# Converting float64 weights beside attention: sign of the weights, centring and the second weight matrix moved to other engines and another time

## The chip, the cores and the metric

The kernel runs on one core of one Trainium2 chip. Its time is the device time of one execution in microseconds (us), taken as the median of several runs. PE is the matrix engine, DVE is VectorE, ACT is ScalarE, POOL is GpSimd, SP is the engine that issues most DMAs.

## The reference

Threshold attention is followed by a Fourier mixing layer and a channel MLP. Everything is float32 but the two weight matrices, which arrive as float64.

```python
# q, k, v: (8 batches, 8 heads, 576 rows, 64);  tau: one number
scores = (q @ k.T) / sqrt(64)
scores = where(scores >= max(scores) - tau, scores, -1e9)
attn = softmax(scores) @ v                       # per head
x = attn, heads side by side                     # (8, 576, 512)
u = x + real(fft(fft(x, axis=1), axis=2))
un = (u - mean(u)) / sqrt(var(u) + 1e-6)         # over the 512 channels
out = u + relu(un @ w_ch1) @ w_ch2               # w_ch1 (512, 2048), w_ch2 (2048, 512), float64
```

## The kernel before, in words

**Attention** is a loop over 160 row steps `i`: 8 batches of 20 steps, a batch being 4 pairs of heads (`n`) with 5 row tiles (`t`) each, four of 128 rows and one of 64. A step has these parts. `scores(i)`: PE computes the scores of both heads into PSUM (`sc`, L319), VectorE takes the negated row maximum (`neg`, L332) and the threshold (`thr`, L336), ScalarE takes the exponential (`e`, L342), VectorE masks it and sums the row (L345), adds 1e-9 and inverts the sum (`den`, L349 and L352), and GpSimd repeats the inverse along a tile (`rec`, L354). `transposed_weights(i - 1)`: PE transposes the previous step's `e` and `rec` (L387, L392, L393), and ScalarE copies them out of PSUM. At the end of a pair `weighted_values` multiplies with the values (L409, L416) and GpSimd folds the rows for the Fourier transform (`fold`, L433 to L435). `e` and `rec` have two buffers.

**Mixing and channels.** After each batch, `mixing(b)` does the Fourier transforms as matmuls with tables of cosines and sines (`dim_c`, `dim_s`, `seq_c`, `seq_s`), and GpSimd adds the result to `x` into a ring `u_t` of two slots of 576 columns (L509 to L513). `channels(g)` then handles groups of 384 rows: 64 matmuls with `w1` (`ph`, L561), ReLU into `h0` to `h3`, a transpose of the rows for the mean and variance (`pn`), and 48 matmuls with `w2` (`po`, L582). This work is cut into units and handed out by `fill()`, three times a step during the next batch, by a budget of matmul columns; what is left runs at the end.

**Weights.** `weights()` is a generator over 32 chunks of 128 x 512: 16 of `w1` (four column groups `g` of four row blocks `c`), then 16 of `w2`. Each step takes two chunks (L640), so the program has them all handed out in the first 16 or 17 steps. `load_weights` reads a chunk as pairs of 32-bit words and builds the float32 value: VectorE masks the mantissa bits (L225), ScalarE makes 1 + mantissa of them (L228), VectorE adds the low word (L229), VectorE cuts out the exponent (L234), ScalarE shifts its bias and place (L238), VectorE puts the sign bit on (L241), and GpSimd multiplies the mantissa by this signed power of two (L245). The staging tiles, 128 x 1536, lie in the four `h` buffers, which `channels` uses later.

**Centring.** After each column group of `w1`, `center(g)` lets PE compute the column mean (`pm`, L253), ScalarE copies it (`mean`, L257), and VectorE subtracts it from each of the four blocks (L264). Blocks with odd `c` are mirrored first by a matmul (`pr`, L262), so VectorE reads those from PSUM.

**Start.** SP issues the loads of the first pair (`load_pair(0)`, 13 DMAs) and of `tau`; VectorE derives four scalars from `tau` (L142 to L154). `load_dim` loads the table `dim_raw`, in one of the two `e` buffers, by two DMAs on GpSimd's queue (L175, L177), and VectorE copies it in 25 pieces into `dim_c` and `dim_s` (L179 to L189).

The order within each engine's queue is chosen by a scheduler over the whole program, by its own model of times; it isn't the order of the source.

Of the kernel before, what the change touches and what calls it, by code (L numbers as in the profile page):

```python
# [9 lines left out]
FP32 = mybir.dt.float32  # L10
INT32 = mybir.dt.int32
UINT32 = mybir.dt.uint32
# [35 lines left out]
def kernel(  # L48
# [44 lines left out]
    def load_pair(n):  # L93
        b, p = n // NPAIR, PAIRS[n % NPAIR]
        hs = [2 * p + (j + p) % 2 for j in range(2)]
        qt = sb.tile([128, NT, 2, D], FP32, tag="q", bufs=1, name="q_in")
        kt = sb.tile([128, NT, 2, D], FP32, tag="k", bufs=1, name="k_in")
        vt = sb.tile([128, 9, D], FP32, tag="v", name="v_in")
        for j, h in enumerate(hs):
            nc.sync.dma_start(  # L100
                out=qt[:, 0:4, j, :], in_=q[b, h, 0:512, :].rearrange("(t p) d -> p t d", p=128)
            )
            nc.sync.dma_start(out=qt[0:64, 4, j, :], in_=q[b, h, 512:576, :])


        h = hs[0]
        nc.sync.dma_start(
            out=kt[:, 0:4, 0, :], in_=k[b, h, 0:512, :].rearrange("(t p) d -> p t d", p=128)
        )
        nc.sync.dma_start(out=kt[0:64, 4, 0, :], in_=k[b, h, 512:576, :])  # L110
        h = hs[1]
        nc.sync.dma_start(out=kt[0:64, 0, 1, :], in_=k[b, h, 512:576, :])
        rows = k[b, h, 0:512, :].rearrange("(t r p) d -> p r t d", r=2, p=64)
        nc.sync.dma_start(out=kt[64:128, 0:4, 1, :], in_=rows[:, 0])
        nc.sync.dma_start(out=kt[0:64, 1:5, 1, :], in_=rows[:, 1])

        for j, h in enumerate(hs):
            nc.sync.dma_start(
                out=vt[:, j:8:2, :], in_=v[b, h, 0:512, :].rearrange("(t p) d -> p t d", p=128)
            )  # L120
            nc.sync.dma_start(out=vt[64 * j : 64 * j + 64, 8, :], in_=v[b, h, 512:576, :])
        loaded[n] = (qt, kt, vt)

    load_pair(0)

# [12 lines left out]

    tau_t = const.tile([128, 1], FP32, name="tau_t")
    nc.sync.dma_start(out=tau_t[:, :], in_=tau.partition_broadcast(128))  # L140
    q_scale = const.tile([128, 1], FP32, name="q_scale")
# [48 lines left out]

    load_dim()

    w1 = [const.tile([128, HID], FP32, name=f"w1_{c}") for c in range(ND)]
# [17 lines left out]

    def load_weights(n, src, dst):

        if src.dtype == FP32:
            nc.sync.dma_start(out=dst, in_=src)
            return
        stage = sb.tile([128, 3 * WC], INT32, tag=f"h{n % 4}", bufs=1, name="stage")
        raw = stage[:, 0 : 2 * WC]
        power = stage[:, 2 * WC : 3 * WC]
        nc.sync.dma_start(out=raw, in_=src.bitcast(INT32))  # L220
        pairs = raw.rearrange("p (n two) -> p n two", two=2)
        low, high = pairs[:, :, 0].bitcast(UINT32), pairs[:, :, 1]
        bits = dst.bitcast(INT32)
# [5 lines left out]
        nc.vector.scalar_tensor_tensor(  # L229
            out=dst, in0=low, scalar=2.0**-52, in1=dst, op0=ALU.mult, op1=ALU.add  # L230
        )


        nc.vector.tensor_scalar(  # L234
            out=power, in0=high, scalar1=20, scalar2=0x7FF,
            op0=ALU.logical_shift_right, op1=ALU.bitwise_and,
        )
        nc.scalar.activation(  # L238
            out=power, in_=power, func=ACT.Relu, bias=shift[:, :], scale=float(1 << 23)
        )  # L240
        nc.vector.scalar_tensor_tensor(  # L241
            out=power, in0=high, scalar=-(1 << 31), in1=power,
            op0=ALU.bitwise_and, op1=ALU.bitwise_or,
        )
        nc.gpsimd.tensor_tensor(out=dst, in0=dst, in1=power.bitcast(FP32), op=ALU.mult)  # L245

    def center(g):
# [8 lines left out]
        mean = sb.tile([128, WC], FP32, tag="u", bufs=3, name="mean")  # L256
        nc.scalar.copy(mean[:, :], pm[:, :])  # L257
        for c in range(ND):
            rows = w1[c][:, cols]
            if c % 2:  # L260
                pr = ps.tile([128, 512], FP32, tag="mm", name="pr")
                nc.tensor.matmul(pr[:, :], mirror[:, :], rows, start=True, stop=True)  # L262
                rows = pr[:, :]
            nc.vector.tensor_tensor(  # L264
                out=w1[c][:, cols], in0=rows, in1=mean[:, :], op=ALU.subtract
            )

    def weights():
        n = 0
        for g in range(HID // WC):  # L270
            cols = slice(WC * g, WC * (g + 1))
            for c in range(ND):
                load_weights(n, w_ch1[128 * c : 128 * (c + 1), cols], w1[c][:, cols])
                n += 1
                yield
            center(g)
        for j in range(NJ):
            load_weights(n, w_ch2[128 * j : 128 * (j + 1), :], w2[j][:, :])
            n += 1
            yield  # L280
# [253 lines left out]
    def channels(g):  # L534
# [23 lines left out]
        for j in range(NJ):  # L558
# [15 lines left out]
            if j == 11:  # L574
                nc.scalar.activation(
                    out=rstd[:, :], in_=mv[:, :, 1], func=ACT.Sqrt, bias=eps[:, :], scale=1.0
                )
                nc.vector.reciprocal(rstd[:, :], rstd[:, :])
        for t in range(nt):
            po = ps.tile([128, DM], FP32, tag="mm", name="po")  # L580
# [47 lines left out]
    for i in range(total + 1):  # L628
# [9 lines left out]
        if i > 0 and t == 0:  # L638
            weighted_values(n - 1)
        for _ in itertools.islice(chunks, 2):  # L640
            pass
# [61 lines left out]
```

## Time and profile before

| | |
|---|---|
| median of 7 runs | 1923.44 us (1921.28 to 1925.78) |
| profiled execution | 1922.82 us, span 1921.0 us |
| mean granted TensorE clock | 0.975 |
| busy: PE, DVE, ACT, POOL | 1844.2, 869.4, 612.3, 237.1 us |

The span runs from the first to the last instruction that the profiler recorded. A group of instructions is shown as line, engine, operation, output and input tiles with partitions x elements and type, count, then busy us and the mean ns of one, then the idle time just before them on that engine and which instruction ended it. In a view of the timeline the first number is the start in us from the span's start and the second the length in us. Busy times of different engines overlap.

### The profile page before, as it was taken

How to read it: one execution, taken by the hardware profiler on the slowest of the kernel's cores; microseconds unless marked ns; L12 is line 12 of the kernel's file. 1: busy time of each engine (PE TensorE's matmuls, PEld its weight loads, DVE VectorE, ACT ScalarE, POOL GpSimd, SP SyncE). 2: the span in 40 equal slices, each digit the busy share in tenths (PEclk: the TensorE clock that was granted, in tenths of full speed). 3: DMA queues.
4: the chain of work that ended last, by engine and by line, in shares of the span. 5: the costliest groups of instructions: out<-in, count | busy, mean ns of one | idle time of the engine just before them, and what ended most of it. 6: DMA issues, size and time to landing. Idle time of an engine off the chain costs nothing.

```text
span 1921.0 us, 20963 instructions
## 1 busy us (share of the span) xinstructions
PE 1844.2 (96%) x7840; PEld 992.6 (52%) x7840; DVE 869.4 (45%) x2015; ACT 612.3 (32%) x1110; POOL 237.1 (12%) x438
## 2 busy tenths in 40 slices
PE   5877899999999999999999999999999999999999
PEld 3444555455455555545455455545555455545454
DVE  6998554533334545443333445544434355431010
ACT  3554443333223334323223234322323233421010
POOL 3433201010000210011000020002000020001000
PEclk9877899999999999999999999999999999999999
DMA  5432100100010010110001010101000001000000
GB/s 154 136 111 75 25 19 19 37 18 19 11 27 23 25 25 14 31 30 7 19 24 23 14 31 13 32 23 25 13 26 17 24 19 25 1 11 6 11 6 16
DMA packets 129701, 56.97 MB, mean 30 GB/s; under 512 B 120677, under 2 KB 120678, under 8 KB 129600
## 3 DMA queue, kind: packets, MB, share of 16 engines
q1 hardware_dynamic: 129232, 54.71, 10.7%
q8 instruction: 62, 1.02, 0.2%
q0 software_dynamic: 368, 0.93, 0.2%
q14 instruction: 39, 0.32, 0.1%
HBM read 46.02 MB, written 9.44 MB: 29 GB/s over the span
## 4 chain that ended last, share of the span: by engine, by line
PE 85%; DVE 10%; ACT 1%; POOL 1%; issue 1%; SPq 0%; DMA 0%; DVEq 0%; ACTq 0%
PE po L582 26%; PE ph L561 25%; PE sc L319 10%; PE pv L409 7%; PE pw L387 6%; PE pa L491 3%; PE pt L296 2%; DVE neg L332 2%; PE pv L416 2%; PE py L474 2%; DVE e L345 2%; DVE stage L241 1%; DVE w L229 1%; PE pe L392 1%; DVE w L225 1%
## 5 line engine op out<-in xcount | busy, mean ns | idle before, releaser
L582 PE MATMUL po<-w,h 128*128 128x512 f32 x1152 | 539.5, 606 | 0.0
L561 PE MATMUL ph<-u_t,w 128*128 128x384 f32 x1536 | 528.7, 493 | 5.4 <-DVE h L569 3.3
L342 ACT ACTIVATE e<-sc,neg 128x576 f32<-128x576 f32 (+1 forms) x320 | 229.2, 740 | 582.9 <-DVE neg L332 579.3
L561 PEld LDWEIGHTS ph<-u_t,w 128*128 128x128 f32 x1536 | 280.7, 190 | 207.3 <-issue 22.5
L332 DVE TENSOR_REDUCE neg<-sc 128x1 f32<-128x576 f32 (+1 forms) x320 | 229.6, 750 | 331.3 <-PE sc L319 330.9
L582 PEld LDWEIGHTS po<-w,h 128*128 128x128 f32 x1152 | 204.9, 190 | 229.8 <-issue 224.4
L319 PE MATMUL sc<-kT,qT 64*128 64x288 f32 (+1 forms) x1280 | 260.0, 450 | 35.9 <-ACT e_t L390 19.3
L345 DVE SCALAR_TENSOR_TENSOR e<-sc,thr,e 128x576 f32<-128x576 f32 (+1 forms) x320 | 250.7, 813 | 30.2 <-ACT e L342 12.7
L319 PEld LDWEIGHTS sc<-kT,qT 64*128 64x128 f32 (+1 forms) x1280 | 128.6, 183 | 167.3 <-issue 95.9
L390 ACT COPY e_t<-pw 128x1024 f32<-128x1024 f32 (+1 forms) x160 | 148.3, 927 | 160.1 <-PE pw L387 154.9
L354 POOL COPY rec<-den 128x128 f32<-128x128 f32 (+1 forms) x160 | 49.9, 312 | 1101.3 <-DVE den L352 932.5
L387 PEld LDWEIGHTS pw<-ident,e 128*128 128x128 f32 (+1 forms) x1280 | 141.6, 146 | 72.3 <-issue 55.1
L387 PE MATMUL pw<-ident,e 128*128 128x128 f32 (+1 forms) x1280 | 168.3, 275 | 0.1
L567 ACT ACTIVATE h<-ph 128x384 f32<-128x384 f32 x96 | 47.2, 492 | 314.7 <-PE ph L561 314.7
L569 DVE TENSOR_SCALAR h<-ph 128x384 f32<-128x384 f32 x96 | 53.3, 555 | 185.2 <-PE ph L561 184.9
L420 DVE TENSOR_TENSOR x<-pv,ends 128x288 f32<-128x288 f32 x64 | 29.2, 457 | 191.1 <-PE pv L416 174.4
L589 DVE SCALAR_TENSOR_TENSOR u<-po,rstd,u 128x512 f32<-128x512 f32 x36 | 27.0, 750 | 157.2 <-PE po L582 157.2
L409 PE MATMUL pv<-e_t,v_in 128*64 128x288 f32 x512 | 72.1, 419 | 0.0
L409 PE MATMUL pv<-e_t,v_rev 128*64 128x288 f32 x512 | 71.3, 418 | 0.1
L394 ACT COPY ends<-pe 128x256 f32<-128x256 f32 (+1 forms) x160 | 57.1, 357 | 3.0 <-PE pe L393 3.0
L409 PEld LDWEIGHTS pv<-e_t,v_in 128*64 128x64 f32 x512 | 34.8, 138 | 37.7 <-issue 10.3
L409 PEld LDWEIGHTS pv<-e_t,v_rev 128*64 128x64 f32 x512 | 34.5, 138 | 37.1 <-issue 11.1
(98 smaller groups left out, 1262.7 us busy)
## 6 DMA issues: line engine op xcount, KB each, us to landing
stage<-in_moe_w_ch_dram SPq DMA_DIRECT2D x32, 512.0 KB, 4.1
out_dram<-u SPq DMA_DIRECT2D x36, 256.0 KB, 2.0
q_in<-in_q_dram SPq DMA_DIRECT2D x64, 128.0 KB, 2.4
v_in<-in_v_dram SPq DMA_DIRECT2D x64, 128.0 KB, 2.4
k_in<-in_k_dram SPq DMA_DIRECT2D x32, 128.0 KB, 2.4
k_in<-in_k_dram SPq DMA_DIRECT2D x64, 64.0 KB, 2.4
q_in<-in_q_dram SPq DMA_DIRECT2D x64, 16.0 KB, 2.4
k_in<-in_k_dram SPq DMA_DIRECT2D x64, 16.0 KB, 2.1
```

What stands on the lines that cost most here:

```text
L319: nc.tensor.matmul(sc[j][0:m, c, 0:HALF], qT[hp, 128 * t : 128 * t + m], kT[hp, HALF * c : HALF * (c + 1)], start=True, stop=True,)
L332: nc.vector.tensor_reduce(out=neg[0:m, j : j + 1], in_=sc[j][0:m, :, 0:HALF], axis=AXIS_XY, op=ALU.max, negate=True,)
L342: nc.scalar.activation(out=ej, in_=sc[j][0:m, :, 0:HALF], func=ACT.Exp, bias=neg[0:m, j : j + 1], scale=1.0)
L345: nc.vector.scalar_tensor_tensor(out=ej, in0=sc[j][0:m, :, 0:HALF], scalar=thr[0:m, j : j + 1], in1=ej, op0=ALU.is_ge, op1=ALU.mult, accum ...
L387: nc.tensor.transpose(pw[:, 4 * j + c, 0:m], e[0:m, c0 : c0 + 128], ident[0:m, 0:m])
L390: nc.scalar.copy(e_t[:, :, qs], pw[:, :, 0:m])
L394: nc.scalar.copy(ends[:, :, qs], pe[:, 0:2, 0:m])
L409: nc.tensor.matmul(pv[64 * j : 64 * j + 64, 0:HALF], vt[:, 2 * c + j, :], e_t[:, 4 * j + c, cols], start=(c == 0), stop=False, skip_group_ ...
L491: nc.tensor.matmul(pa[0:m, 0:KH], y[0:n, u, cols], table[0:n, u, :], start=(u == 0), stop=(u == 2),)
L561: nc.tensor.matmul(ph[:, 0:GT], w1[c][:, 128 * j : 128 * (j + 1)], u_t[:, c, c0 : c0 + GT], start=(c == 0), stop=(c == ND - 1),)
L569: nc.vector.tensor_relu(ht, ph[:, 0:GT])
L582: nc.tensor.matmul(po[:, :], hT[j // 4][:, j % 4, 128 * t : 128 * (t + 1)], w2[j][:, :], start=(j == 0), stop=(j == NJ - 1),)
```

## The change

1. **Sign.** VectorE no longer puts the sign bit on. GpSimd multiplies the mantissa by the unsigned power of two, ScalarE computes Sign of the high word (`high`, in place, as float32), and GpSimd multiplies by that in a second operation. The power now lies in the words of `low`, so a staging tile is 128 x 1024.
2. **Centring.** ScalarE stores the negated mean. For odd blocks PE adds it to the mirrored block by a second matmul into `pr`, and ScalarE copies the sum to `w1`. For even blocks GpSimd adds it.
3. **When.** A step takes one chunk in the first 20 steps and two after that. A `w2` chunk is staged in the second slot of the ring `u_t` (two buffers), no longer in the `h` buffers. Before its `w2` matmuls, `channels` takes what chunks are left.
4. **Queues and tables.** `tau` and the five loads of the first pair's `k` are issued by ScalarE. `load_dim` is called in step 7, no longer ahead of the loop.

```diff
@@ -96,6 +96,8 @@
         qt = sb.tile([128, NT, 2, D], FP32, tag="q", bufs=1, name="q_in")
         kt = sb.tile([128, NT, 2, D], FP32, tag="k", bufs=1, name="k_in")
         vt = sb.tile([128, 9, D], FP32, tag="v", name="v_in")
+
+        k_queue = nc.sync if n else nc.scalar
         for j, h in enumerate(hs):
             nc.sync.dma_start(
                 out=qt[:, 0:4, j, :], in_=q[b, h, 0:512, :].rearrange("(t p) d -> p t d", p=128)
@@ -104,15 +106,15 @@
 
 
         h = hs[0]
-        nc.sync.dma_start(
+        k_queue.dma_start(
             out=kt[:, 0:4, 0, :], in_=k[b, h, 0:512, :].rearrange("(t p) d -> p t d", p=128)
         )
-        nc.sync.dma_start(out=kt[0:64, 4, 0, :], in_=k[b, h, 512:576, :])
+        k_queue.dma_start(out=kt[0:64, 4, 0, :], in_=k[b, h, 512:576, :])
         h = hs[1]
-        nc.sync.dma_start(out=kt[0:64, 0, 1, :], in_=k[b, h, 512:576, :])
+        k_queue.dma_start(out=kt[0:64, 0, 1, :], in_=k[b, h, 512:576, :])
         rows = k[b, h, 0:512, :].rearrange("(t r p) d -> p r t d", r=2, p=64)
-        nc.sync.dma_start(out=kt[64:128, 0:4, 1, :], in_=rows[:, 0])
-        nc.sync.dma_start(out=kt[0:64, 1:5, 1, :], in_=rows[:, 1])
+        k_queue.dma_start(out=kt[64:128, 0:4, 1, :], in_=rows[:, 0])
+        k_queue.dma_start(out=kt[0:64, 1:5, 1, :], in_=rows[:, 1])
 
         for j, h in enumerate(hs):
             nc.sync.dma_start(
@@ -121,6 +123,8 @@
             nc.sync.dma_start(out=vt[64 * j : 64 * j + 64, 8, :], in_=v[b, h, 512:576, :])
         loaded[n] = (qt, kt, vt)
 
+    tau_t = const.tile([128, 1], FP32, name="tau_t")
+    nc.scalar.dma_start(out=tau_t[:, :], in_=tau.partition_broadcast(128))
     load_pair(0)
 
 
@@ -136,8 +140,6 @@
 
 
 
-    tau_t = const.tile([128, 1], FP32, name="tau_t")
-    nc.sync.dma_start(out=tau_t[:, :], in_=tau.partition_broadcast(128))
     q_scale = const.tile([128, 1], FP32, name="q_scale")
     nc.vector.tensor_scalar(
         out=q_scale[:], in0=tau_t[:], scalar1=0.0, scalar2=SCALE, op0=ALU.is_ge, op1=ALU.mult
@@ -188,8 +190,6 @@
                     c, f, n = c + 1, f + step, n - 1
                 nc.vector.tensor_copy(dim_s[:, c : c + n], _stepped(raw, 256 + f, step, n))
 
-    load_dim()
-
     w1 = [const.tile([128, HID], FP32, name=f"w1_{c}") for c in range(ND)]
     w2 = [const.tile([128, DM], FP32, name=f"w2_{j}") for j in range(NJ)]
 
@@ -209,17 +209,18 @@
     shift = const.tile([128, 1], FP32, name="shift")
     nc.vector.memset(shift[:], -float((1023 - 127) << 23))
 
-    def load_weights(n, src, dst):
+    def load_weights(src, dst, raw):
+
 
         if src.dtype == FP32:
             nc.sync.dma_start(out=dst, in_=src)
             return
-        stage = sb.tile([128, 3 * WC], INT32, tag=f"h{n % 4}", bufs=1, name="stage")
-        raw = stage[:, 0 : 2 * WC]
-        power = stage[:, 2 * WC : 3 * WC]
-        nc.sync.dma_start(out=raw, in_=src.bitcast(INT32))
-        pairs = raw.rearrange("p (n two) -> p n two", two=2)
-        low, high = pairs[:, :, 0].bitcast(UINT32), pairs[:, :, 1]
+        nc.sync.dma_start(
+            out=raw, in_=src.bitcast(INT32).rearrange("p (c n) -> p c n", c=2)
+        )
+        pairs = raw.rearrange("p c (n two) -> p c n two", two=2)
+        low, high = pairs[:, :, :, 0], pairs[:, :, :, 1]
+        dst = dst.rearrange("p (c n) -> p c n", c=2)
         bits = dst.bitcast(INT32)
 
         nc.vector.tensor_scalar(
@@ -227,22 +228,21 @@
         )
         nc.scalar.activation(out=dst, in_=bits, func=ACT.Copy, bias=1.0, scale=2.0**-20)
         nc.vector.scalar_tensor_tensor(
-            out=dst, in0=low, scalar=2.0**-52, in1=dst, op0=ALU.mult, op1=ALU.add
+            out=dst, in0=low.bitcast(UINT32), scalar=2.0**-52, in1=dst, op0=ALU.mult, op1=ALU.add
         )
 
 
         nc.vector.tensor_scalar(
-            out=power, in0=high, scalar1=20, scalar2=0x7FF,
+            out=low, in0=high, scalar1=20, scalar2=0x7FF,
             op0=ALU.logical_shift_right, op1=ALU.bitwise_and,
         )
         nc.scalar.activation(
-            out=power, in_=power, func=ACT.Relu, bias=shift[:, :], scale=float(1 << 23)
-        )
-        nc.vector.scalar_tensor_tensor(
-            out=power, in0=high, scalar=-(1 << 31), in1=power,
-            op0=ALU.bitwise_and, op1=ALU.bitwise_or,
-        )
-        nc.gpsimd.tensor_tensor(out=dst, in0=dst, in1=power.bitcast(FP32), op=ALU.mult)
+            out=low, in_=low, func=ACT.Relu, bias=shift[:, :], scale=float(1 << 23)
+        )
+        nc.gpsimd.tensor_tensor(out=dst, in0=dst, in1=low.bitcast(FP32), op=ALU.mult)
+        sign = high.bitcast(FP32)
+        nc.scalar.activation(out=sign, in_=high, func=ACT.Sign)
+        nc.gpsimd.tensor_tensor(out=dst, in0=dst, in1=sign, op=ALU.mult)
 
     def center(g):
 
@@ -254,29 +254,32 @@
                 pm[:, :], ones[:, :], w1[c][:, cols], start=(c == 0), stop=(c == ND - 1)
             )
         mean = sb.tile([128, WC], FP32, tag="u", bufs=3, name="mean")
-        nc.scalar.copy(mean[:, :], pm[:, :])
+        nc.scalar.mul(mean[:, :], pm[:, :], -1.0)
         for c in range(ND):
             rows = w1[c][:, cols]
             if c % 2:
                 pr = ps.tile([128, 512], FP32, tag="mm", name="pr")
-                nc.tensor.matmul(pr[:, :], mirror[:, :], rows, start=True, stop=True)
-                rows = pr[:, :]
-            nc.vector.tensor_tensor(
-                out=w1[c][:, cols], in0=rows, in1=mean[:, :], op=ALU.subtract
-            )
+                nc.tensor.matmul(pr[:, :], mirror[:, :], rows, start=True, stop=False)
+                nc.tensor.matmul(pr[:, :], ident[:, :], mean[:, :], start=False, stop=True)
+                nc.scalar.copy(rows, pr[:, :])
+            else:
+                nc.gpsimd.tensor_tensor(out=rows, in0=rows, in1=mean[:, :], op=ALU.add)
 
     def weights():
         n = 0
         for g in range(HID // WC):
             cols = slice(WC * g, WC * (g + 1))
             for c in range(ND):
-                load_weights(n, w_ch1[128 * c : 128 * (c + 1), cols], w1[c][:, cols])
+                stage = sb.tile([128, 2, WC], INT32, tag=f"h{n % 4}", bufs=1, name="stage")
+                load_weights(w_ch1[128 * c : 128 * (c + 1), cols], w1[c][:, cols], stage[:, :, :])
                 n += 1
                 yield
             center(g)
+
         for j in range(NJ):
-            load_weights(n, w_ch2[128 * j : 128 * (j + 1), :], w2[j][:, :])
-            n += 1
+            c = 2 * (j % 2)
+            raw = u_t[:, c : c + 2, S : S + WC].bitcast(INT32)
+            load_weights(w_ch2[128 * j : 128 * (j + 1), :], w2[j][:, :], raw)
             yield
 
 
@@ -576,6 +579,8 @@
                     out=rstd[:, :], in_=mv[:, :, 1], func=ACT.Sqrt, bias=eps[:, :], scale=1.0
                 )
                 nc.vector.reciprocal(rstd[:, :], rstd[:, :])
+        for _ in chunks:
+            pass
         for t in range(nt):
             po = ps.tile([128, DM], FP32, tag="mm", name="po")
             for j in range(NJ):
@@ -637,7 +642,9 @@
         fill()
         if i > 0 and t == 0:
             weighted_values(n - 1)
-        for _ in itertools.islice(chunks, 2):
+        if i == 7:
+            load_dim()
+        for _ in itertools.islice(chunks, 1 if i < per_batch else 2):
             pass
         if i > 0 and i % per_batch == 0:
             b = i // per_batch - 1
```

## The prediction

> **What bounds the kernel now.** I read the page's shares and its 40 slices first, to see whether one engine bounds the whole span.
>
> ```profile
> PE 1844.2 (96%) x7840; PEld 992.6 (52%) x7840; DVE 869.4 (45%) x2015; ACT 612.3 (32%) x1110; POOL 237.1 (12%) x438
> ...
> PE   5877899999999999999999999999999999999999
> ...
> DVE  6998554533334545443333445544434355431010
> ```
>
> A slice is 48 us. PE is full from the sixth slice on; only in the first four (195 us) is it not, and there VectorE shows 6, 9, 9, 8. All that the change touches lies in these slices and the one or two behind them, so the second view is the windows over that stretch.
>
> ```profile
> core 0: us, PE busy (x) PEld busy (x) DVE busy (x) ACT busy (x) POOL busy (x), PEclk, DMA share, GB/s
> 0.00:50.00 50.00, 29.68 (x95) 16.81 (x96) 35.18 (x95) 20.07 (x31) 17.11 (x33) 0.93 0.56 154
> 50.00:100.00 50.00, 42.77 (x175) 22.45 (x173) 49.23 (x103) 28.39 (x46) 20.09 (x21) 0.87 0.48 141
> 100.00:150.00 50.00, 36.86 (x150) 21.02 (x150) 47.00 (x94) 26.02 (x42) 18.53 (x18) 0.68 0.36 109
> 150.00:195.00 45.00, 34.77 (x162) 20.66 (x161) 36.91 (x76) 22.17 (x35) 14.53 (x16) 0.75 0.24 65
> 195.00:250.00 55.00, 50.48 (x252) 30.51 (x254) 28.75 (x68) 20.86 (x39) 11.70 (x21) 0.88 0.08 17
> 250.00:300.00 50.00, 49.80 (x263) 28.53 (x262) 28.34 (x69) 21.59 (x43) 4.24 (x11) 1.00 0.09 19
> ```
>
> VectorE is busy 49.2 of 50 us, then 47.0 of 50: the first batch (20 row steps) is VectorE's. Up to 195 us it works 168.3 us, ScalarE 96.7, GpSimd 70.3, and PE idles 50.9. From 250 us on PE has no room. A microsecond saved on VectorE before 195 us is a microsecond off the span as long as nothing else is late; one saved after 250 us is nothing. The timeline puts the first `neg` (L332) of step 1 at 16.9, of step 16 at 170.8 and of step 20 at 194.9 us: with conversions a step takes 10.3 us, without them (steps 16 to 19) 6.0.
>
> The third view is the groups of lines up to 195 us.
>
> ```profile
> L241 DVE SCALAR_TENSOR_TENSOR stage<-stage 128x512 int32<-128x512 int32 x32 | 29.3, 916 | 0.0
> L229 DVE SCALAR_TENSOR_TENSOR w<-stage,w 128x512 f32<-128x512 uint32 x32 | 23.3, 728 | 0.8 <-ACT w L228 0.7
> L234 DVE TENSOR_SCALAR stage<-stage 128x512 int32<-128x512 int32 x32 | 22.8, 714 | 0.0
> L225 DVE TENSOR_SCALAR w<-stage 128x512 int32<-128x512 int32 x32 | 19.0, 593 | 0.4 <-DMA stage<-in_moe_w_ch_dram 0.4
> L264 DVE TENSOR_TENSOR w<-w,mean 128x512 f32<-128x512 f32 x8 | 5.4, 679 | 0.4 <-ACT mean L257 0.4
> L264 DVE TENSOR_TENSOR w<-pr,mean 128x512 f32<-128x512 f32 x8 | 5.4, 678 | 0.0
> ...
> L245 POOL TENSOR_TENSOR w<-w,stage 128x512 f32<-128x512 f32 x32 | 46.6, 1456 | 57.6 <-DVE stage L241 44.7 <-DVE den L352 12.9
> ...
> L238 ACT ACTIVATE stage<-stage,shift 128x512 int32<-128x512 int32 x32 | 22.9, 716 | 18.3 <-DVE stage L234 14.4 <-DMA stage<-in_moe_w_ch_dram 2.3 <-DVE den L352 0.9
> ```
>
> These means hide a second length. In the timeline of VectorE and GpSimd around 30 us:
>
> ```profile
> 30.46 1.64 POOL L245 TENSOR_TENSOR w<-w,stage 128x512 f32<-128x512 f32 x1 [0.62 <-DVE stage L241]
> ...
> 30.90 1.48 DVE L234 TENSOR_SCALAR stage<-stage 128x512 int32<-128x512 int32 x1
> ...
> 32.64 0.41 DVE L234 TENSOR_SCALAR stage<-stage 128x512 int32<-128x512 int32 x1
> ```
>
> The same L234 takes 0.41 us when GpSimd is free and 1.48 us beside its multiplication: VectorE is held until GpSimd ends. So GpSimd's work has a price on VectorE, and the change gives GpSimd twice as much of it.
>
> **The sum, part by part.** Times go against the profiled execution (1922.8 us, span 1921.0; the median of the runs, 1923.4, is 0.6 above). In the instruction order of the changed kernel as built, PE, VectorE, ScalarE and GpSimd run as before from about step 25 on, so only the first 250 us can differ.
>
> *Off VectorE.* Sign insertion L241, 29.3 us; centring L264, 10.8; and the w2 chunks that leave the first batch. That order moves only five of the 16 past step 20 (w2_11 to w2_15); eleven are still converted in the first batch. Five times 593 + 714 + 728 ns is 10.2. Together −50.3.
>
> *More holding by GpSimd.* Each chunk now has two multiplications, and centring adds 8 additions: in the first batch 27 × 2 + 8 = 62 operations for 32. At 1456 ns that is 90 us for 46.6; of a first batch of 154 us before and some 135 after, the share goes from 0.30 to 0.67, 2.2 times. The holds that remain exposed are those on L234, 32 × (714 − 410) = 9.7, L225, 32 × (593 − 410) = 5.9, and L229, 32 × (728 − 680) = 1.5 (medians 418, 422 and 680 ns): 17.1, for 27 chunks 14.4. Times 2.2 is 31.7: +17, and +2 for `thr` (211 ns free, mean 279): +19. No hold growing gives 0; each operation holding as now, 0.83 us, gives +35 (rival B).
>
> *GpSimd's own queue.* `rec` (L354), for which PE's transpose of it (L393) waits each step, now queues behind two multiplications: up to 1.5 us more a step, 29 us in all. Its cover is PE's 50.9 us of idle time: 0, and if it is gone, those 29.
>
> *PE, ScalarE.* Eight matmuls more, by L262's eight (16 records, 9.1 us busy), in the same idle time: 0. ScalarE gets 32 Signs, of which no row shows one; bounds from L228 (627) and L238 (716 ns) are 20 to 23 us, and 8 PSUM copies at L257's 581 ns, 4.6: 97 becomes 125 of some 180 us. It is not the bound: 0. If Sign needed another table than Exp, each pair of switches would be 2 × 1.28 us (ACT_TABLE_LOAD L305); the built order has no second load before the first batch ends: 0.
>
> *Start.* The `tau` wait on VectorE (10.5 us) goes, but the first L225, L229 and L234 now stand ahead of step 0's `neg` and wait for the first weight load, which SP still issues: 0, ±2.
>
> *dim table at step 7.* The 24 copies are moved, same cost. `dim_raw` takes one of the two `e` buffers and has two DMAs on GpSimd's queue with 4.0 us to landing; VectorE's copies wait behind them, then the next steps' `e`: up to 8 us, the DMA alone 4: +4.
>
> *Loads.* L225 of chunk n needs the load into the buffer that GpSimd's last multiplication of chunk n−4 frees; that is later now, and a load takes 4.1 us. 0 to 10: +4.
>
> *Second batch.* w2_11 to w2_15 use the unused half of `u_t`. GpSimd's two multiplications of w2_11 stand among mixing's additions into `u_t`, for which PE's L561 waits already (0.94 us after L513): 2 × 1.46 + 0.6 = 3.5. PE waits for ScalarE's Sign of w2_12 to w2_15: 1. The loads of w2_14 and w2_15 wait for GpSimd, and their L225 stands ahead of step 25's `e` on VectorE, on which PE then waits: 4.1 + 1.5 less what is queued, 5. Bounds 3 to 20: +10, all on a full PE.
>
> Sum: −50.3 + 19 + 4 + 4 + 10 = −13.3, so 1909.5 profiled, 1910 as a median.
>
> A rule speaks against this: the Trainium skill, "Perfetto Trace Analysis", section "Optimizing Scalar/DVE Operations", says that GpSimd and VectorE share an SBUF read port, so that moving work between the two might not help. The held L234 agrees. By it alone the sign and GpSimd's half of centring would win nothing; 5.4 + 10.2 would be left against 18 of waits, about +2: no change. I stay with the rows: L241 costs 916 ns each, and a hold falls only on instructions that meet it.
>
> **Rivals.** *A, more is won.* VectorE, with 50 us less, stops being the bound, and what is held no longer ends last: holds +0 to +5 and the rest as above, −50.3 + 3 + 18 = −29, 1894. For it: VectorE's load falls to some 120 of 180 us, and steps without conversions take 6.0 us. Against it: 62 GpSimd operations of 1.5 us fall on 20 steps, three to a step.
>
> *B, slower: GpSimd's holding eats the gain.* In the first batch each GpSimd operation now holds VectorE 26.4 / 32 = 0.83 us (17.1, L241's 32 × (916 − 670) = 7.9, `thr` 1.4). With h per operation the sum is −50.3 + 62h − 15.8 + 18: zero at h = 0.78, slower beyond doubt from 0.84; the long hold above is 1.07. At 0.9 it is +8, 1931; at 1.07, +18. For it: before's own 0.83. Against it: fewer instructions can be hit, as L241, the longest, is gone; my forecast is h = 0.56.
>
> *C, the moved chunks give nothing,* and waits in the second batch reach 20: −50.3 + 19 + 8 + 20 = −3, 1920: no change.
>
> **How the numbers follow.** About 0.2% (3.8 us) is what a measurement of this kernel tells from no change. Forecast 0.50 (its own range 1902 to 1917), A 0.20, B 0.22, C 0.08. Faster is forecast and A, 0.70; same 0.08; slower 0.22. The range leaves out the lower half of A and the upper half of B: 1895 to 1931.
>
> **What would show it.** Right: step 20's first `neg` at 165 to 175 us instead of 194.9; L234's and L225's means above 800 and 700 ns; GpSimd above 60% in the windows to 150 us; PE waits of some 10 us between 200 and 250 us, at L561 and behind step 25's `e`. A shows in means that stay as they are and step 20 before 162 us; B in step 20 after 180 us; C in step 20 as forecast, with PE's idle time in the second batch doubled. Wrong at the root: ACT_TABLE_LOADs between Exp and Sign, an order of time different after 260 us, or PE's wait for `rec` as the largest in the first batch.

## The result and the profile after

The changed kernel takes 1932.04 us (median of 16 runs, 1926.51 to 1941.9), against 1923.54 for the kernel before: a ratio of 1.0049, 95% interval 1.004 to 1.0059. It is 9 us slower where 13 us faster was forecast. The profiled execution takes 1931.84 us, its span is 1930.1. In what follows an effect is the ratio's distance from 1 times 1923 us, and a place in a kernel is timed by the first `neg` of a step, counted from the span's start.

On the page, in the 40 slices (48 us each):

```profile
PE   6678889999999999999999999999999999999999
...
DVE  6976556444243455444334445543334355531010
...
POOL 4764230110000110011000020002000020001000
```

VectorE falls to 7 and 6 in the third and fourth slice, as meant (9 and 8 before), but PE hardly rises with it (7 and 8, for 7 and 7), falls from 8 to 6 in the second, and shows 8 in the sixth, where it had 9. In the windows over the same stretches as in the prediction:

```profile
0.00:50.00 50.00, 31.44 (x113) 19.22 (x114) 33.88 (x75) 26.50 (x42) 22.03 (x38) 0.90 0.64 177
50.00:100.00 50.00, 33.77 (x160) 18.92 (x158) 49.89 (x98) 31.75 (x53) 40.31 (x35) 0.83 0.42 124
100.00:150.00 50.00, 36.42 (x158) 20.95 (x160) 36.91 (x71) 29.04 (x47) 29.79 (x27) 0.77 0.19 54
150.00:195.00 45.00, 38.59 (x176) 21.21 (x174) 30.19 (x65) 23.77 (x40) 17.18 (x21) 0.80 0.30 85
195.00:250.00 55.00, 46.35 (x195) 27.15 (x195) 27.97 (x64) 20.00 (x37) 15.13 (x22) 0.78 0.10 26
250.00:300.00 50.00, 47.13 (x244) 26.77 (x244) 31.14 (x76) 25.67 (x52) 14.88 (x19) 1.00 0.15 40
```

Three things are to be seen. From 50 to 100 us VectorE is full (49.89) with fewer instructions, and GpSimd is busy 40.31 of 50 us. From 100 to 195 us VectorE is no longer full (67.1 of 95 us) and yet nothing is faster. From 195 to 300 us PE lacks 6.8 us of what it worked before. Step 20 begins at 192.7 us (194.9 before), step 28 at 283.5 (272.2): the first batch gained 2.2 us, the eight steps behind it lost 13.4, and 2.1 came back later.

The groups of VectorE up to 195 us that were lengthened:

```profile
L230 DVE SCALAR_TENSOR_TENSOR w<-stage,w 128x512 f32<-128x512 uint32 x16 | 20.1, 1257 | 1.1 <-ACT w L229 1.1
L235 DVE TENSOR_SCALAR stage<-stage 128x512 int32<-128x512 int32 x16 | 12.2, 761 | 0.2
L226 DVE TENSOR_SCALAR w<-stage 128x512 int32<-128x512 int32 x16 | 11.5, 723 | 5.7 <-DMA stage<-in_moe_w_ch_dram 5.7
L352 DVE TENSOR_SCALAR den<-den 128x2 f32<-128x2 f32 (+1 forms) x20 | 10.2, 512 | 0.2
```

L230 (L229 before) was 728 ns and is 1257, and 842 for the eleven chunks staged in `u_t`; L352 (L349 before), on two numbers a row, was 157 and is 512. The timelines of VectorE and GpSimd show how one instruction comes to be held over several operations:

```profile
49.84 0.68 DVE L230 SCALAR_TENSOR_TENSOR w<-stage,w 128x512 f32<-128x512 uint32 x1
...
52.98 0.41 DVE L235 TENSOR_SCALAR u_t<-u_t 128x512 int32<-128x512 int32 x1
...
54.65 4.40 DVE L230 SCALAR_TENSOR_TENSOR w<-stage,w 128x512 f32<-128x512 uint32 x1
58.97 1.24 DVE L339 TENSOR_SCALAR thr<-neg,thr_off 128x2 f32<-128x2 f32 x1
```

```profile
49.72 3.82 POOL L357 COPY rec<-den 64x128 f32<-64x128 f32 x1 [0.56 <-DVE den L355]
53.51 1.29 POOL L245 TENSOR_TENSOR w<-w,stage 128x512 f32<-128x512 f32 x1
54.76 2.49 POOL L266 TENSOR_TENSOR w<-w,mean 128x512 f32<-128x512 f32 x2
57.22 1.27 POOL L242 TENSOR_TENSOR w<-w,stage 128x512 f32<-128x512 f32 x1
58.57 1.61 POOL L245 TENSOR_TENSOR w<-w,stage 128x512 f32<-128x512 f32 x1
```

L230 stands for 4.40 us while GpSimd runs three operations back to back (54.76 to 58.49), and ends 0.56 us after the third. It works the other way too: `rec` on GpSimd, 0.28 us at its shortest, stands for 3.82 us from 49.72 while VectorE runs eight instructions of conversions without a gap (49.84 to 53.39).

### The profile page after: what moved, and what is told of

It is laid out like the page before. It is cut to its first block, busy times and chain, and to the rows that moved or that the text cites. A ratio compares the mean times of both kernels' runs of the same rounds, so it can differ in the third digit from the quotient of the medians.

```text
span 1930.1 us, 21086 instructions
## 1 busy us (share of the span) xinstructions
PE 1841.8 (95%) x7856; PEld 991.2 (51%) x7856; DVE 857.9 (44%) x1967; ACT 634.1 (33%) x1150; POOL 290.2 (15%) x478
## 3 DMA queue, kind: packets, MB, share of 16 engines
q1 hardware_dynamic: 129904, 54.41, 10.6%
## 4 chain that ended last, share of the span: by engine, by line
PE 80%; DVE 4%; POOL 1%; ACT 1%; issue 1%; DMA 0%; DVEq 0%; ACTq 0%; POOLq 0%
PE po L587 26%; PE ph L564 25%; PE sc L322 9%; PE pv L412 6%; PE pw L390 5%; PE pa L494 3%; PE pt L299 2%; PE pv L419 2%; PE py L477 2%; DVE neg L335 1%; DVE e L348 1%; PE pe L395 1%; PE pe L396 1%; PE pn L548 1%; DVE s L454 0%
## 5 line engine op out<-in xcount | busy, mean ns | idle before, releaser
L564 PEld LDWEIGHTS ph<-u_t,w 128*128 128x128 f32 x1536 | 281.6, 191 | 215.4 <-issue 24.3
L322 PE MATMUL sc<-kT,qT 64*128 64x288 f32 (+1 forms) x1280 | 248.5, 453 | 40.5 <-DVE e L348 26.6
L348 DVE SCALAR_TENSOR_TENSOR e<-sc,thr,e 128x576 f32<-128x576 f32 (+1 forms) x320 | 250.8, 813 | 32.8 <-ACT e L345 14.9
L322 PEld LDWEIGHTS sc<-kT,qT 64*128 64x128 f32 (+1 forms) x1280 | 122.4, 184 | 165.8 <-issue 115.6
```

The lines of the kernel that those rows point to most:

```text
L322: nc.tensor.matmul(sc[j][0:m, c, 0:HALF], qT[hp, 128 * t : 128 * t + m], kT[hp, HALF * c : HALF * (c + 1)], start=True, stop=True,)
L348: nc.vector.scalar_tensor_tensor(out=ej, in0=sc[j][0:m, :, 0:HALF], scalar=thr[0:m, j : j + 1], in1=ej, op0=ALU.is_ge, op1=ALU.mult, accum ...
L564: nc.tensor.matmul(ph[:, 0:GT], w1[c][:, 128 * j : 128 * (j + 1)], u_t[:, c, c0 : c0 + GT], start=(c == 0), stop=(c == ND - 1),)
```

## How the first batch was taken apart

Between the first `neg` of step 0 and that of step 20, VectorE's time in the trace's records falls into three: *held* (by which an instruction is longer than the lower quartile of its line and operation), *clean* (the rest of its busy time) and *idle*. "Step 20" is when it begins, against 194.9 us before; "20 to 28" is what these eight steps take more than before (77.3 us). "Chunks" is how many of the 32 conversions begin before step 20 in VectorE's order of instructions.

| kernel | chunks | clean | held | idle | step 20 | 20 to 28 | ratio (95%) |
|---|---|---|---|---|---|---|---|
| before | 32 | 138.6 | 27.3 | 14.1 | | | 1 |
| changed | 27 | 105.8 | 40.2 | 30.2 | -2.2 | +13.4 | 1.0049 (1.004 to 1.0059) |
| e1 sign | 32 | 120.0 | 47.8 | 10.2 | -2.0 | +0.3 | 0.999 (0.9979 to 1.0002) |
| e2 centring | 32 | 129.2 | 31.9 | 15.4 | -3.3 | 0 | 0.9997 (0.9987 to 1.0006) |
| e3 schedule | 21 | 118.9 | 6.1 | 18.9 | -36.1 | +13.5 | 0.9911 (0.9892 to 0.9929) |
| e4 queues, table | 32 | 139.4 | 19.3 | 18.4 | -1.8 | +1.9 | 0.9987 (0.9978 to 0.9995) |
| e5 all but sign | 26 | 116.8 | 16.1 | 30.9 | -14.0 | +8.6 | 0.9974 (0.9957 to 0.9992) |
| e6 thin sign | 27 | 105.4 | 24.3 | 27.0 | -22.2 | +8.6 | 0.9939 (0.9924 to 0.9955) |
| e7 all, pinned | 18 | 95.4 | 23.9 | 36.9 | -22.7 | +39.4 | 1.0073 (1.0059 to 1.0088) |
| e8 all but schedule | 32 | 112.3 | 40.5 | 26.0 | +0.1 | -0.2 | 0.9997 (0.9986 to 1.0009) |
| e9 all but centring | 25 | 111.0 | 28.8 | 21.9 | -17.3 | +16.6 | 0.9986 (0.9976 to 0.9997) |
| e10 schedule, queues | 22 | 117.4 | 9.1 | 21.4 | -30.5 | +14.4 | 0.9914 (0.99 to 0.9927) |
| e11 schedule, centring | 26 | 118.9 | 20.0 | 30.6 | -10.5 | +6.2 | 0.9971 (0.996 to 0.9981) |
| e12 same, without GpSimd | 27 | 121.6 | 15.5 | 29.9 | -12.9 | +5.0 | 0.9995 (0.9983 to 1.0008) |
| e13 e11 held back | 21 | 110.9 | 17.7 | 29.4 | -21.9 | +23.7 | 1.0035 (1.0022 to 1.0048) |
| e14 all, held back | 21 | | | | | | 1.0048 (1.0036 to 1.006) |
| e15 schedule, pinned | 18 | 114.1 | 7.4 | 29.1 | -29.4 | +30.2 | 1.0006 (0.9994 to 1.0017) |
| e16 schedule, sign | 25 | 111.7 | 27.8 | 21.6 | -18.9 | +16.9 | 1.0002 (0.999 to 1.0015) |
| e17 four buffers | 27 | 106.1 | 40.1 | 32.1 | -0.9 | +13.9 | 1.0055 (1.0041 to 1.0068) |
| e18 all but sign, centring | 21 | 116.3 | 7.0 | 26.7 | -28.4 | +19.3 | 0.9956 (0.9942 to 0.997) |

The ratios are from timed runs, the other columns from one profiled execution each, which may stand some us off the median (e3's took 1898.1 us, its median is 1905.3). e14 has no usable profile, only the order of its instructions and its timed runs.

## Experiments: one part alone

**e1**, the kernel before with the sign moved:

```diff
-        nc.vector.scalar_tensor_tensor(
-            out=power, in0=high, scalar=-(1 << 31), in1=power,
-            op0=ALU.bitwise_and, op1=ALU.bitwise_or,
-        )
         nc.gpsimd.tensor_tensor(out=dst, in0=dst, in1=power.bitcast(FP32), op=ALU.mult)
+        sign = high.bitcast(FP32)
+        nc.scalar.activation(out=sign, in_=high, func=ACT.Sign)
+        nc.gpsimd.tensor_tensor(out=dst, in0=dst, in1=sign, op=ALU.mult)
```

> The kernel before with the sign alone moved to ScalarE and a second GpSimd multiplication. Theory H (GpSimd's holding of VectorE eats the gain): -29.3 us on VectorE against 32 more GpSimd operations; at the 0.83 us per operation of the kernel before the sum is -29.3 + 64 x 0.83 - 18.5 = +5 us, and L234's and L225's means rise above 0.9 us. Theory W (the gain of the sign is real, and the loss comes from new waits for loads and from the second batch): holding at 0.6 us per operation, -29.3 + 38 - 18.5 = -10 us, give or take 4.

-2 us, and the interval holds no change: between the two theories. VectorE's clean time falls by 18.6 us, and held time rises by 20.5, to 47.8: 0.75 us for each of the 64 multiplications, between H's 0.83 and W's 0.6. Taking the 29.3 us of L241 off VectorE bought nothing, as VectorE spends it waiting for the GpSimd that does the work instead.

**e2**, the kernel before with `center` as changed.

> The kernel before with the centring alone taken off VectorE (half to PE and ScalarE, half to GpSimd). Both theories: -10.8 us on VectorE and 8 more GpSimd operations. H: 8 x 0.83 = 6.6 us given back, -4 us. W: 8 x 0.6 = 5 us given back, -6 us. A result at or above zero would say that PE or ScalarE queue delays count in the first batch.

No change (0.9997): both theories missed. Step 20 comes 3.3 us earlier (clean -9.4, held +4.6), which the end doesn't show.

**e3**, the changed kernel with sign, centring, queues and table put back, which leaves

```diff
-        for _ in itertools.islice(chunks, 2):
+        for _ in itertools.islice(chunks, 1 if i < per_batch else 2):
```

and the staging of `w2` in `u_t`.

> The kernel before with the later, thinner schedule of the chunks alone (one chunk a step, w2 staged in the second slot of u_t, two buffers). The sign stays on VectorE, the centring too. W: the moved chunks make waits for loads in VectorE's queue and wait in the second batch, about 10 us there and 5 to 10 us in the first batch, against 5 x 2.95 = 15 us off VectorE before step 20: between 0 and +8 us, slower than before. H: no more GpSimd work in the first batch, so -15 + 10 = -5 us.

-17 us, outside both. The prediction had given the schedule five moved chunks; built alone it moves eleven, and VectorE is no longer saturated, and held time falls from 27.3 to 6.1 us, more than the chunks' share. The second batch gives back 13.5 of the 36.1 us. In the windows of e3, VectorE is nowhere full:

```profile
50.00:100.00 50.00, 42.80 (x233) 25.76 (x232) 44.76 (x103) 28.04 (x46) 17.50 (x19) 0.88 0.33 95
100.00:150.00 50.00, 42.41 (x197) 24.08 (x194) 42.40 (x98) 25.20 (x40) 18.42 (x22) 0.85 0.24 66
```

**e4**, the changed kernel with all but queues and table put back.

> The changed kernel with sign, centring and schedule of the chunks put back: what is left of the change is tau and the first k on ScalarE's queue and the dim table at step 7. Both theories: -2 to +4 us; the start gains nothing as the first neg comes at 15 to 16.5 us, and the table at step 7 costs up to 4 us of VectorE's time by its load.

-2.5 us, just past the lower end.

So the four parts alone give -2, 0, -17 and -2.5, together +9. What the rest had to find is why they don't add up.

## Experiments: one part taken back, or made cheap

**e5**, the changed kernel with the sign on VectorE (the first diff, reversed).

> The changed kernel with the sign put back on VectorE; the order of instructions still has 26 of 32 chunks ahead of step 20 (the changed kernel 27, the schedule alone in e3 21). Theory G (the second GpSimd multiplication is what costs, by holding VectorE and by freeing the staging buffers late): without it the other parts show what they gave alone, -17.8 + 0.6 - 3 = about -20 us against the kernel before. Theory P (what costs is the crowding of w2 chunks into the first batch, which the order shows): still about the time of the changed kernel, 0 to +8 us.

-5 us, between the two. The sign's move thus costs 14 us in this company, but without it the other parts give 15 less than their sum.

**e6**, the changed kernel with a narrow second multiplication:

```diff
-        nc.gpsimd.tensor_tensor(out=dst, in0=dst, in1=sign, op=ALU.mult)
+        nc.gpsimd.tensor_tensor(out=dst[:, :, 0:1], in0=dst[:, :, 0:1], in1=sign[:, :, 0:1], op=ALU.mult)
```

> The changed kernel, with the second multiplication (sign) on only one column of each half of a chunk, so that most weights stay without their sign; Sign on ScalarE stays whole. The order of the chunks is nearly that of the changed kernel (27 ahead of step 20). Theory G: its 32 x 1.3 us on GpSimd gone, holds on VectorE fall by half and the second batch's chain by 1.3 us a chunk: -15 to -25 us against the kernel before. Theory P: the crowding stays, at most 5 us better than the changed kernel, so 0 to +5.

-12 us, at the edge of G's range; the second multiplication costs 21 us. The order being nearly the same, the table shows where: clean time is equal (105.4 and 105.8), held time is 15.9 us less, idle 3.2 less. Against e5 (-5 us) it also says what L241 was worth: with the second multiplication narrow, though not free (0.27 to 0.41 us each), taking L241 off VectorE gains 7 us at the end, not 29.

**e8**, the changed kernel with two chunks a step and `w2` staged in the `h` buffers.

> The changed kernel with two chunks a step and w2 staged in the h buffers as before: sign, centring and queues changed, all 32 chunks in the first batch. If the parts add up, -2 + 0.6 - 3 = -4 us. If GpSimd's 72 operations in the first batch hold VectorE as in the changed kernel (0.6 us each) without a gain from moved chunks: -40.1 + 43 - 18.5 + waits of 4 to 13 = -12 to -2 us. Above zero it would say that the schedule of the chunks isn't what makes the changed kernel slow.

No change (-0.6 us): neither the parts' sum nor a loss. Held time, 40.5 us, is as in the changed kernel.

**e9**, the changed kernel with the centring on VectorE.

> The changed kernel with the centring put back on VectorE; 25 chunks stand ahead of step 20. The second multiplication's price, 21 us between e6 and the changed kernel, is there whole. If centring off VectorE is what spoils the change: below e5, -10 us or better against the kernel before. If the second multiplication is, in whatever company: 0 to +8 us.

-2.7 us, just below the second range: neither as good as e5 or better, nor as slow as the changed kernel. Idle time is 8 us less than there, held 11.

## Experiments: two parts together

Each is e3 with one more part; e18 is the changed kernel with sign and centring put back.

**e10**, with the queues.

> The schedule of the chunks with tau and the first k on ScalarE's queue, and nothing else of the change; 22 chunks ahead of step 20. Theory C (crowding: every chunk kept ahead of step 20 costs some 3 us of VectorE, and loads into two buffers are waited for): as e3, -17 us, and 1 to 3 better by the queue, -20. Theory S (the queues and the table at step 7 are what makes e5 12 us slower than e3): clearly worse than e3, -5 to -10.

-16.5 us, as e3: the queues add nothing.

**e18**, with queues and table.

> The schedule of the chunks with the queues and the table at step 7: the whole change but sign and centring; 21 chunks ahead of step 20. If these parts add up: -17 and -2.5, about -20 us. If what e10 showed holds (nothing added): -16 to -18. Worse than -14 would say that the table at step 7 costs here what it did not cost in e4.

-8.5 us: the table at step 7, harmless in e4, costs 8 us here (to e10), most of it after step 20, where 19.3 us are lost for 14.4.

**e16**, with the sign.

> The schedule of the chunks and the sign on ScalarE and GpSimd, and nothing else of the change; 25 chunks ahead of step 20. Against e3 it prices the sign in the company of the schedule. Theory C and G together: as e9, which has the queues and the table besides, -3 us. If the queues and the table were what spoils e9: -10 to -17.

No change, just above the first theory's -3: with the sign moved, and the four more chunks that the scheduler then puts ahead of step 20 (25 for 21), all 17 us of the schedule are gone. Held time is 27.8 us for 6.1; clean time is 7.2 less, so it isn't the four chunks' own work.

**e11**, with the centring as changed.

> The schedule of the chunks with the centring off VectorE as changed, sign on VectorE, queues and table as before; 26 chunks ahead of step 20, as in e5. Theory C: VectorE's 10.8 us are spent on five more chunks in the first batch and their waits: about e5, -5 us, though the centring alone cost nothing. Theory S: as e3 or better, -17 to -22.

-5.6 us: as theory C has it.

**e12**, with all blocks centred by PE and ScalarE:

```diff
-            if c % 2:
-                pr = ps.tile([128, 512], FP32, tag="mm", name="pr")
-                nc.tensor.matmul(pr[:, :], mirror[:, :], rows, start=True, stop=False)
-                nc.tensor.matmul(pr[:, :], ident[:, :], mean[:, :], start=False, stop=True)
-                nc.scalar.copy(rows, pr[:, :])
-            else:
-                nc.gpsimd.tensor_tensor(out=rows, in0=rows, in1=mean[:, :], op=ALU.add)
+            pr = ps.tile([128, 512], FP32, tag="mm", name="pr")
+            turn = mirror if c % 2 else ident
+            nc.tensor.matmul(pr[:, :], turn[:, :], rows, start=True, stop=False)
+            nc.tensor.matmul(pr[:, :], ident[:, :], mean[:, :], start=False, stop=True)
+            nc.scalar.copy(rows, pr[:, :])
```

> As e11, but all eight even blocks are centred by PE and ScalarE as the odd ones are, so that GpSimd gets nothing more than before; 27 chunks ahead of step 20. Against e11 it tells GpSimd's additions (8 x 1.37 us, of which 0.56 is held: some 6 us) from the crowding. Theory C: -5 to -10. If GpSimd's additions are the cause in e11: as e3, -17 or better.

No change, a smaller gain than either range: GpSimd's eight additions are not what e11 loses against e3.

## Experiments: the place of the chunks, and the buffers

In e11, e12 and e5 the scheduler, with less on VectorE, puts 26 or 27 chunks ahead of step 20 where e3 has 21. e13 to e15 and e7 hold chunks back by a copy ahead of a chunk's load, from a tile that the step makes:

```diff
+            if j >= 5:
+                nc.gpsimd.tensor_copy(u_t[0:1, c, S : S + 1], pinned[0][0:1, 0:1])
             load_weights(w_ch2[128 * j : 128 * (j + 1), :], w2[j][:, :], raw)
...
+        if i in steps:
+            pinned[0] = steps[i][1]
         for _ in itertools.islice(chunks, 1 if i < per_batch else 2):
```

**e13**, e11 with this.

> e11 (schedule and centring), with the loads of w2_5 and later waiting for the step that hands them out, so 21 chunks stand ahead of step 20, as in e3. Theory C (crowding): five chunks less in the first batch, 3.3 us each, 16 us off it, and 6 to 10 back in the second: -11 to -20 us against the kernel before, where e11 had -5. Theory K (the centring's own waits): as e11, -5, or worse.

+7 us: against theory C, and within K's "or worse". Five chunks fewer bring step 20 forward by 11.4 us, 2.3 each, so crowding is real. But the eleven chunks now crowd steps 20 to 27, and 23.7 us are lost there for 6.2. Held and idle time stay at 17.7 and 29.4, against 6.1 and 18.9 in e3 with as many chunks. The held time goes with the centring: e15 below, which holds chunks back without it, has 7.4. The idle time need not: e15 has 29.1, so holding back alone brings as much.

**e14**, the changed kernel with this.

> The whole change, with w2_5 and later held back in the same way, so 21 chunks ahead of step 20 and 11 behind. Theory C: step 20 some 20 us earlier than in the changed kernel; the second batch takes eleven chunks with two GpSimd multiplications each and gives back more than the 13 us that five cost: e7 gave back 39 for 14. So step 20 at -20 against before and the end between -5 and +10. Theory K: step 20 as in the changed kernel, and the end worse than it, +12 or more.

+9 us, as the changed kernel; it fits C's range, but without a usable profile it doesn't tell the two apart.

**e15**, e3 with every `w2` chunk held (without the condition on `j`).

> e3 (the schedule alone), with all w2 loads waiting for the step that hands them out: 18 chunks ahead of step 20 for 21. If VectorE's time stays the price in the first batch: three chunks more leave it, 10 us, and the second batch takes them for 1.2 us each (13.5 us for eleven in e3): -24 us against the kernel before. If the second batch has no room left: -10 to -17.

No change, outside both: 30.2 us are lost from step 20 to 28, for 13.5 in e3. But step 20 itself comes 6.7 us later than in e3 with three chunks fewer ahead of it, and idle time is 10.2 us more: the holding back has a price of its own. Whether the second batch had no room left for three chunks more, or their late loads cost the time, isn't shown; the same holds for e7, e13 and e14.

**e7**, the changed kernel with every `w2` chunk held.

> The changed kernel whole, but each w2 load waits (by a copy of one number from rec of its step) for the step in which the program hands the chunk out; so 18 chunks stand ahead of step 20 and 14 behind. Theory P: nine chunks leave the first batch, some 27 us off it, and 10 to 14 come back in the second: -10 to -18 us against the kernel before. Theory G: the GpSimd work moves to where its end stands on PE's way (additions into u_t, rec), so no better than the changed kernel: +5 to +12.

+14 us, against theory P and above G's range: 39.4 us are lost in the eight steps from 20 on.

**e17**, the changed kernel with four buffers for `w2` up to w2_10:

```diff
-            raw = u_t[:, c : c + 2, S : S + WC].bitcast(INT32)
+            s0 = S if j >= 11 or j // 2 % 2 else 0
+            raw = u_t[:, c : c + 2, s0 : s0 + WC].bitcast(INT32)
```

> The changed kernel, with the w2 chunks up to w2_10 staged in turn in both slots of u_t, four buffers for two; the order of the chunks on VectorE stays the same (27 ahead of step 20). If the waits for loads count: L226's 9 us of waiting go, step 20 comes 6 to 9 us earlier and the end with it: 0 to +3 us against the kernel before, where the changed kernel has +9. If they only stand in for GpSimd's queue, which is as long as before: +7 to +10.

+10.6 us, as the changed kernel, and the wait is still there (9.0 us in the changed kernel). In e17's waits of VectorE from 15 to 195 us:

```profile
DVE w L226 <- DMA u_t<-in_moe_w_ch_dram: 12.0, 4, 5.3
```

This doesn't clear the buffers, as the trace shows no four buffers at work. GpSimd's second multiplications of w2_2 and w2_4, and SP's issues of the loads of w2_4 and w2_6 (counted in order of time; the last line merges two issues):

```profile
116.76 1.74 POOL L245 TENSOR_TENSOR w<-w,u_t 128x512 f32<-128x512 f32 x1
...
133.18 1.51 POOL L245 TENSOR_TENSOR w<-w,u_t 128x512 f32<-128x512 f32 x1
```

```profile
118.53 0.57 SPq L218 DMA_DIRECT2D u_t<-in_moe_w_ch_dram  x1
...
134.71 5.66 SPq L218 DMA_DIRECT2D u_t<-in_moe_w_ch_dram  x2
```

Each load leaves at most 0.03 us after the last multiplication of the chunk two before. With four buffers w2_4 would have to wait for w2_0 alone, which GpSimd had done at 67.1 us. Eight of the ten loads from w2_2 to w2_11 start in this way, the same eight as in the changed kernel. Why the built program still waits for the chunk two before isn't shown, and what four buffers would give stays untested.

In the changed kernel the 9.0 us are three waits, 2.36, 5.18 and 1.47 us, for the loads of w2_4, w2_6 and w2_10. The longest, on GpSimd, SP and VectorE:

```profile
132.89 1.57 POOL L245 TENSOR_TENSOR w<-w,u_t 128x512 f32<-128x512 f32 x1
```

```profile
134.48 5.66 SPq L218 DMA_DIRECT2D u_t<-in_moe_w_ch_dram  x2
```

```profile
138.49 1.31 DVE L226 TENSOR_SCALAR w<-u_t 128x512 int32<-128x512 int32 x1 [5.18 <-DMA u_t<-in_moe_w_ch_dram]
```

All three loads start at most 0.03 us after GpSimd's last multiplication of the chunk two before, and take 4.0 to 4.3 us. So VectorE waits for loads that wait for GpSimd.

## Right and wrong, step by step

**The bound** was read rightly for the kernel before: VectorE bounds the first batch (PE's fifth slice, at 8, was passed over). But that a microsecond saved on VectorE before 195 us is one off the span did not hold once chunks moved: e13 reaches step 20 21.9 us earlier and ends 7 us later.

**The sum of the first batch** is the step that failed, by 21 us: step 20 was forecast at 171.6 (194.9 - 50.3 + 19 + 8) and came at 192.7. Against before, clean time is -32.8, held +12.9, idle +16.1, and the start +1.6. The forecast in the same terms: its -50.3 holds 10.6 us of holds (L241's 7.9 and those of the five chunks, 5 x 535 ns), so clean -39.7, held +8.4, idle +8. All three terms were too favourable:

- *Off VectorE, -50.3.* Clean time is 6.9 us too much. One cause can be read off: L241 lasts 0.67 us but the next instruction starts 0.60 after it, so means add up to more than the time. And the credit was not the path's: for L241 29.3 us were booked, while e1 took 18.6 us of clean time off and got 20.5 of held time back, and e5 to e6, with the second multiplication narrow, gains 7 us.
- *Holding, +19,* was 4.5 too low. Per GpSimd operation it is 40.2 / 62 = 0.65 us for my 0.56. That the total came so near is in part luck, as the holds fell elsewhere. The sum scaled up mainly those on L234 and L225; measured over the first batch, L234's are 9.1 us (9.7 before) and L225's 7.1 (5.8 before), and their means up to 195 us, 751 and 671 ns, stay below the 800 and 700 that were named as signs. The growth is on L229 (11.1 us for 1.7), on `thr` (4.6 for 1.3) and on the first operation on `den` (7.1 for 0.1), which the sum didn't have. Holding is the mechanism that undoes the sign: e5 to the changed kernel, clean -11.0, held +24.1, and 14 us at the end; e6 gives 16 us of held time back in nearly the same order.
- *New waits, +8,* was 8 too low: VectorE is idle 30.2 us for 14.1. The *Loads* term (+4, at most 10) was right in its mechanism and too small: L226 waits 9.0 us for loads that start when GpSimd has freed their buffer (under e17), for 0.4 before. The dim table's +4 doesn't appear as a wait of VectorE. Of the rest, waits for PE's scores grow from 5.6 to 9.2 us and those for ScalarE's `e` from 2.9 to 4.8, of which the sum had nothing. Of the kernels with the new schedule and no chunk held back, those with the centring off VectorE have 27 to 32 us of idle time (changed, e5, e6, e11, e12, e17), those with it on VectorE 19 to 22 (e3, e9, e10, e16) and 27 (e18); the centring had been booked as a pure gain of 10.8. It isn't one wait: from step 0's `neg` to step 20's, VectorE waits 5.3 us for scores and 0.3 for `w2` loads in e3, 10.8 and 6.4 in e11, 13.2 and 1.8 in e12, 6.0 and 9.4 in e5. As these also have 26 or 27 chunks ahead of step 20 for 21, what part is the centring's own isn't shown.

**Second batch, +10:** 13.4 to step 28, 2.1 of it gained back later; right in its mechanism. The chain of waits of the changed kernel runs as the prediction said it would, here its longer pieces:

```profile
249.86 0.44 DVE u_t L235
...
250.38 0.77 ACT u_t L239
...
252.59 1.35 POOL w L245
253.94 1.26 POOL w L242
...
255.27 1.29 POOL w L245
...
256.58 4.24 DMA u_t<-in_moe_w_ch_dram
...
261.26 1.55 DVE e L348 x4
...
265.70 0.59 PE ph L564
```

A chunk's multiplications on GpSimd release the load (4.24 us), L226 waits for it ahead of step 25's `e` on VectorE, and PE's `ph` waits behind these. PE's wait for the additions into `u_t`, 0.9 us before, is 5.1.

**At nothing** were booked `rec` (PE waits 3.9 us for it in the first batch, 1.7 before), ScalarE (no second table load: right) and the start (+1.6: inside its bounds). The dim table, +4, costs 8 beside the schedule (e10 to e18) and nothing that shows in e4.

**The five moved chunks** were counted rightly, but their price was not: a chunk ahead of step 20 was booked at 2.0 us. The chunks' means with L241 in its place come to 2.95; where nothing else is moved, eleven bring step 20 forward by 36.1 us, 3.3 each (e3).

**The rivals.** B named the direction of the result, the time (1931) and the engine, and step 20 after 180 us is its mark. Its price per operation, 0.84 us or more, is refuted: at the 0.65 measured its own sum gives -8, so that its time was hit is in part luck. Held time is 12.9 of the 29.0 us by which held and idle time grew together; the idle time and the oversized credit are the rest. A is refuted as the holds did grow. The rule of the Trainium skill ("Perfetto Trace Analysis", "Optimizing Scalar/DVE Operations"), that moving work between VectorE and GpSimd might not help, agrees with these runs: the sign's move gave 2 us alone, which is not told from nothing (e1), and cost 14 and 17 us in company (e5 to the changed kernel, e3 to e16).

**What stays open:** why held time rises with the centring (e11, e12, e13), how much of the idle time is the centring's, what more staging buffers would give, and what makes the table at step 7 cost 8 us.

**A faster kernel** came out: the schedule alone (e3), 0.9911 of the kernel before, and e10 equal to it.

## What to carry to other kernels

Work taken off the bounding engine is worth what the next engine takes in its place: if the two hold each other up in the trace, count held time per operation, and test with the new operation made narrow and the order kept. Parts that are harmless alone can cost together, since each changes where a scheduler puts the others; so count in the built order how many pieces stand in each stage, and price the stage that receives them. A credit summed from mean durations is not what the path gains: here L241's 29.3 us became 7 (e5 to e6), while a chunk's 2.95 became 3.3 (e3). And whether a change relaxes the wait that it is made for is read in the trace: e17's loads still waited for the same instructions.

## What the runs showed of the hardware

- Holding spans several operations: one VectorE instruction of 0.68 us stood 4.40 us while GpSimd ran three back to back. It acts both ways: a copy of 0.28 us on GpSimd stood 3.82 us while VectorE ran eight instructions of conversions without a gap.
- A GpSimd multiplication of 128 x 2 numbers still took 408 ns on `stage` and 271 on `u_t` (e6; 1395 for 128 x 512 on `stage` in the changed kernel), so a narrow one is not free:

```profile
L245 POOL TENSOR_TENSOR w<-w,stage 128x2 f32<-128x2 f32 x16 | 6.5, 408 | 3.6 <-ACT stage L244 2.6
```

- How much is held doesn't follow from GpSimd's time alone: 52 to 55 us of its two-input operations in the first batch held VectorE 27.3 us in the kernel before, 19.3 in e4, 20.0 in e11 and 16.1 in e5, and 34.4 us held it 6.1 in e3. That VectorE's saturation decides is likely, but was not tested by itself.
